# Two VectorE operations instead of three in a weight decode, and a cosine reduced by an integer conversion

## The chip, the cores and the metric

One core of one Trainium2 chip. The metric is the device time of the program in microseconds (us); less is better. A profile of one execution of the kernel before the change is at hand.

## The reference

Three stages follow one another. Attention with a sparse mask runs over 4 batches, 8 heads, 576 positions and 64 columns a head; its output is laid out as 2304 tokens by 512. Two feed-forward layers (512 to 2048 to 512) follow:

```python
h = x @ w_in                      # first layer
x = (h * np.cos(h)) @ w_out
h = x @ w_in2                     # second layer
x = (P(h) / (Q(h) + 1e-6)) @ w_out2
```

P is a cubic in h, Q is 1 + |b0||h| + |b1|h^2. The weights w_in and w_out of both layers reach the chip as 64-bit words (an 8-byte word for each weight), and the kernel turns each word into an fp32 number.

## The kernel before, in words

**Tiling and steps.** A step is one slice of 128 of the 2048 hidden columns for one block of tokens. `l1` (L419) makes h for it with 12 matrix multiplications: the token slices x and the weights are each held as a high and a low part, and high times high, high times low and low times high are summed. `l2` (L438) adds the slice's share of the output with 12 more. The first layer has 128 steps: steps 0 to 31 on two blocks of 256 tokens that alternate, 16 on a block of 352, 80 on five blocks of 288. The second layer has 96 steps of 384 tokens, with another elementwise part (`ew_a` to `ew_d`), which the change does not touch.

**Decode of the weights.** Each weight tile is loaded as `raw` (128 x 512 words of 8 bytes). `dec_abs` lets ScalarE scale the upper half-word, read as fp32, by 2^-112 (L142; one tile, L144, goes to VectorE). `dec_ops` then makes three VectorE operations on 128 x 512: a shift left by 3 (c = 0, L154), the sign bit (c = 1, L156), and the three bits that come from the lower half-word (c = 2, L158). `w_split` makes the high part on ScalarE (L173) and the low part on GpSimd or VectorE (L176). The first layer's 32 tiles are decoded during the start and steps 0 to 15; the second layer's 32 tiles between about 170 and 505 us, and these are written to memory and read back later.

**Elementwise part of the first layer** (`ew_op`), one letter an operation: U or u makes u = h/2pi + 0.25 on ScalarE (L508) or VectorE (L510); K or k copies h out of its bank (L512, L514); J or j adds the number 1.5 x 2^23 on ScalarE (L516) or VectorE (L518), which rounds u to a whole number; V takes the difference of the two (L520, VectorE); N is the sine on ScalarE (L522); M multiplies by h, or by its copy where there is one (L524, VectorE); G and H make the high and low parts (L528, L530) for `l2`.

**What sets the order.** The order is written out by hand: a list of commands for the start (`START`), a string of letters for each step (`ORD`, `C_ORD`), with s and w for the splits of decoded tiles, a and b for `dec_abs` of the next step's tiles, x, y, z, p, q for their `dec_ops` (x is c = 0 of both, y and z are c = 1, p and q are c = 2), T and L for pieces of attention. Each engine works through its own instructions in that order. `l1` is issued at the head of a step, and in the first 32 steps `l2` of a step two steps later. h lies in one of two PSUM banks: `l1` of a step waits until the last reader of h of two steps before is done.

**Attention** for later tokens runs in between, in pieces: transposes (L355), products with v (L374), their copies (L363, L385, L386), sums and normalisations (L297, L344 to L346).

Of the kernel before, what the change touches and what calls it, by code (L numbers as in the profile page):

```python
# [8 lines left out]
F32 = mybir.dt.float32  # L9
F32R = mybir.dt.float32r  # L10
I32 = mybir.dt.int32
BF16 = mybir.dt.bfloat16
AF = mybir.ActivationFunctionType
ALU = mybir.AluOpType
AX = mybir.AxisListType

B, H, S, D = 4, 8, 576, 64
# [3 lines left out]
NF = DFF // 128  # L21
# [12 lines left out]
NB2 = 384  # L34
# [17 lines left out]
LV1 = (3, 4)  # L52
PL1 = []
AB_ORD = "UKjVTswxyzNMabpqGHL"
NEED = {"J": "U", "V": "J", "N": "V", "M": "N", "G": "M", "H": "G"}
REST = "swNMUKjVGhTL"
C_ORD = {}
ORD = {}
for _g in (0, 1, 23):
    ORD[_g] = "ukjVTswxyzNMabpqGHL"  # L60
NPRE = 4
EVB, STB = 4, 6
LATE_OE = False
# [3 lines left out]
NCONST = C_ID + 128  # L67
TWO_PI = 6.2831850
INV_2PI = 1.0 / (2.0 * math.pi)
MAGIC = 12582912.0  # L70
LN_SHIFT = 2.0 ** -63


# [17 lines left out]
def attention_moe_moe_kernel(ctx: ExitStack, tc: tile.TileContext, qk0, qk, vv, w1, w2, consts, a, b, out):  # L91
    nc = tc.nc
    ACT, DVE, POOL, PE, SP = nc.scalar, nc.vector, nc.gpsimd, nc.tensor, nc.sync
# [4 lines left out]
    ep = ctx.enter_context(tc.tile_pool(name="ep", bufs=2))  # L98
# [13 lines left out]
    biases = const.tile([128, 4], F32, name="biases")  # L112
# [16 lines left out]
    def w_load(p, src, key, f, o, ring=False, eng=None):  # L129
        if ring:  # L130
            t = wp.tile([128, 512, 2], I32, tag=f"w{o}", name="raw")
        else:
            t = p.tile([128, 512, 2], I32, tag="A", bufs=ABUFS, name="raw")
        (eng or SP).dma_start(out=t.rearrange("p n w -> p (n w)"), in_=src[f, o].bitcast(I32))
        raws[key, f, o] = t

    def dec_abs(key, f, o, eng=None):
        t = raws.pop((key, f, o))
        m = stage("dec")
        src = t[:, :, 1].bitcast(F32)  # L140
        if eng is None:
            ACT.activation(out=m, in_=src, func=AF.Copy, scale=2.0 ** -112)  # L142
        else:
            eng.tensor_scalar(out=m, in0=src, scalar1=2.0 ** -112, scalar2=None, op0=ALU.mult)  # L144
        return t, m

    def dec_bits(*tms):
        dec_bits1(*tms)
        dec_bits2(*tms)

    def dec_ops(c, t, m):
        mi = m.bitcast(I32)
        if c == 0:
            DVE.tensor_scalar(out=mi, in0=mi, scalar1=3, scalar2=None, op0=ALU.logical_shift_left)  # L154
        elif c == 1:
            DVE.scalar_tensor_tensor(out=mi, in0=t[:, :, 1], scalar=-0x80000000, in1=mi, op0=ALU.bitwise_and, op1=ALU.bitwise_or)  # L156
        else:
            DVE.scalar_tensor_tensor(out=mi, in0=t[:, :, 0], scalar=29, in1=mi, op0=ALU.logical_shift_right, op1=ALU.bitwise_or)  # L158

    def dec_bits1(*tms):  # L160
        for c in (0, 1):
            for t, m in tms:
                dec_ops(c, t, m)

    def dec_bits2(*tms):
        for t, m in tms:
            dec_ops(2, t, m)

    def w_split(m, key, f, o, eng, heng=None):
        w = wp.tile([128, 2, 512], F32R, tag=f"w{o}", name=f"w{o}")  # L170
# [325 lines left out]
    def ew_new(g, bk, h):  # L496
        n = blocks[bk]["n"]
        e = dict(g=g, h=h)
        for k in ("u", "t", "hs"):
            e[k] = ep.tile([128, NB2], F32, tag=k, name=k)[:, :n]  # L500
        for k in ("gh", "gl"):
            e[k] = None
        return e

    def ew_op(c, e):
        u, t, hs, h = e["u"], e["t"], e["hs"], e["h"]
        if c == "U":
            ACT.activation(out=u, in_=h, func=AF.Identity, scale=INV_2PI, bias=biases[:, 2:3])  # L508
        elif c == "u":
            DVE.tensor_scalar(out=u, in0=h, scalar1=INV_2PI, scalar2=0.25, op0=ALU.mult, op1=ALU.add)  # L510
        elif c == "K":
            ACT.activation(out=hs, in_=h, func=AF.Copy)  # L512
        elif c == "k":
            DVE.tensor_copy(out=hs, in_=h)  # L514
        elif c == "J":
            ACT.activation(out=t, in_=u, func=AF.Identity, bias=biases[:, 3:4])  # L516
        elif c == "j":
            DVE.tensor_scalar(out=t, in0=u, scalar1=MAGIC, scalar2=None, op0=ALU.add)  # L518
        elif c == "V":
            DVE.scalar_tensor_tensor(out=u, in0=t, scalar=MAGIC, in1=u, op0=ALU.subtract, op1=ALU.subtract)  # L520
        elif c == "N":
            ACT.activation(out=u, in_=u, func=AF.Sin, scale=-TWO_PI)  # L522
        elif c == "M":
            DVE.tensor_tensor(out=t, in0=u, in1=hs if "K" in e else h, op=ALU.mult)  # L524
        elif c == "G":
            n = t.shape[1]
            e["gh"], e["gl"] = (gp.tile([128, NB2], F32R, tag=k, name=k)[:, :n] for k in ("gh", "gl"))
            ACT.activation(out=e["gh"], in_=t, func=AF.Copy)  # L528
        else:
            (POOL if c == "H" else DVE).tensor_tensor(out=e["gl"], in0=t, in1=e["gh"].bitcast(F32), op=ALU.subtract)  # L530
            state["g", e["g"]] = e["gh"], e["gl"]

# [118 lines left out]
    def order(g):  # L651
        return ORD[g] if g in ORD else AB_ORD if g < 2 * NF else C_ORD[g % (2 * NF)] if g % (2 * NF) in C_ORD else REST
# [9 lines left out]
    def run_steps(p, g0, g1):  # L662
        for g in range(g0, g1):
            bk = None
            if g < len(steps):
                bk, f = steps[g]
                h = l1(bk, f)
            if state["evac"]:
                evac(state["evac"].pop())
            run("early", g)  # L670
            if g < N1:
                todo = decs.pop(g, ())
                e = ew_new(g, bk, h)
                fifo = {c: state["e"] + [e] if c in "NMGH" else [e] for c in "UKJVNMGH"}
                state["e"].append(e)
                for c in order(g):
                    if c.upper() in fifo:
                        for x in fifo[c.upper()]:
                            if c.upper() not in x and NEED.get(c.upper(), "U") in x | {"U": 1}:
                                x[c.upper()] = True  # L680
                                ew_op(c, x)
                                break
                    elif c in "sS":
                        split1(0, POOL if c == "s" else DVE)
                    elif c in "wW":
                        split1(1, POOL if c == "w" else DVE)
                    elif c in "xyzpq":
                        if c == "x":
                            for _, tm in todo:
                                dec_ops(0, *tm)  # L690
                        else:
                            i = "yzpq".index(c)
                            if i % 2 < len(todo):
                                dec_ops(1 + i // 2, *todo[i % 2][1])
                    elif c in "ab":
                        for k in dplan.get(g + 1, ())["ab".index(c):][:1]:
                            w_abs(g + 1, k)
                    elif c == "T":
                        run("pe1", g)
                        run("pe1e", g)  # L700
                    elif c == "L":
                        run("late", g)
                state["e"] = [x for x in state["e"] if "H" not in x]
                state["dec"] = todo
            else:
                for x in state["e"]:
                    for c in "NMGH":
                        if c not in x:
                            ew_op(c, x)
                state["e"] = []  # L710
                second(g, LAG)
                if g == N1:
                    nc.scalar.preload_act_table_set("natural_log_exp_and_others")
                prev = state.pop("prev", None)
                if prev is not None:
                    ew_b(*prev)
                if state["evac"]:
                    evac(state["evac"].pop())
                if bk is not None:
                    state["prev"] = ew_a(p, bk, h)  # L720
                if prev is not None:
                    gh = ew_c(*prev[:2])
                if bk is not None:
                    ew_r(*state["prev"])
                if prev is not None:
                    state["g", g - 1] = ew_d(*prev[:2], gh)
                run("pe1", g)
                run("pe1e", g)
                run("late", g)
            if g < N1:  # L730
                second(g, LAG_AB if bk <= bB else LAG)
            run("pe2", g)
            run("load", g)
# [5 lines left out]
    with tc.manual_schedule():  # L739
        with tc.tile_pool(name="att", bufs=2) as p:  # L740
# [1 line left out]
            DVE.memset(msk16, 0.0)  # L742
            DVE.memset(biases[:, 1:2], -63.0 * math.log(2.0))
            DVE.memset(biases[:, 2:3], 0.25)
            DVE.memset(biases[:, 3:4], MAGIC)
            wb = bank("a")
            ms = {}

# [181 lines left out]
```

## Time and profile before

| what | value |
|---|---|
| median of 3 runs | 993.06 us (992.69 to 993.42) |
| profiled execution | 990.51 us, span 988.7 us, mean granted TensorE clock 0.984 |
| TensorE (PE) busy | 925.2 us, 94% |
| VectorE (DVE) busy | 786.6 us, 80% |
| ScalarE (ACT) busy | 670.8 us, 68% |
| GpSimd (POOL) busy | 287.5 us, 29% |

The page gives busy time over the whole span. Stages have different limits, so the rows further down cut the span at 27, 45, 100, 133, 185.5 and 575 us: the end of the first attention pieces, the first steps, the end of the first layer's decode, the end of the steps of 256 tokens, the end of the first layer. In a row of a group, the number after "x" is how many instructions it holds.

### The profile page before, as it was taken

The page shows a single profiled execution, that of the slowest core. Times are in us where ns is not written, and L with a number is a line of the kernel's source. Part 1 is how long each engine was busy: PE and PEld are TensorE (multiplying, and loading weights), DVE is VectorE, ACT ScalarE, POOL GpSimd, SP SyncE. Part 2 cuts the span into 40 slices and gives each one's busy share as a digit, 9 for nine tenths or more (in the row PEclk, how much of TensorE's full clock was granted, in tenths as well). Part 3 has the DMA queues.
Part 4 walks back from the last instruction along what each step waited for, and adds up shares of the span by engine and source line. Part 5 has one row for each costly group of instructions (what it writes and reads, how often), then busy time and mean ns, then how long its engine had stood idle before and what let it go on. Part 6 is the DMA issues. An engine that isn't in the chain of part 4 may idle for free.

```text
span 988.7 us, 17482 instructions
## 1 busy us (share of the span) xinstructions
PE 925.2 (94%) x6367; PEld 861.8 (87%) x6367; DVE 786.6 (80%) x1497; ACT 670.8 (68%) x1444; POOL 287.5 (29%) x279
## 2 busy tenths in 40 slices
PE   7557889999999989999899999999999999999997
PEld 6557789998999989999899988888888898898896
DVE  5999986688677787777878898877787778777776
ACT  5765557565475565765757887777777777777775
POOL 2466552213212122121222223223223232232221
PEclk9778999999999999999999999999999999999999
DMA  9745200443423534234325620010010100100000
GB/s 312 254 168 216 62 22 9 148 159 109 138 86 128 172 138 160 89 128 151 128 60 178 188 78 1 2 64 1 6 60 1 51 14 1 65 1 0 33 1 32
DMA packets 51526, 89.36 MB, mean 90 GB/s; under 512 B 4584, under 2 KB 28400, under 8 KB 51440
## 3 DMA queue, kind: packets, MB, share of 16 engines
q1 hardware_dynamic: 50720, 86.58, 26.6%
q10 hardware_dynamic: 720, 1.67, 0.5%
q8 instruction: 50, 0.82, 0.3%
q14 instruction: 36, 0.29, 0.1%
HBM read 70.40 MB, written 17.83 MB: 89 GB/s over the span
## 4 chain that ended last, share of the span: by engine, by line
DVE 32%; PE 26%; ACT 22%; POOL 10%; issue 7%; DMA 3%; POOLq 0%; SPq 0%; ACTq 0%; DVEq 0%
PE h L419 11%; PE y L438 10%; POOL z L478 9%; DVE r L481 7%; ACT r L477 6%; ACT r L476 5%; ACT gh L487 4%; DVE h L482 3%; DVE dec L156 3%; DVE a L482 3%; DVE t L524 3%; DVE dec L158 2%; PE a L259 2%; DVE u L520 2%; DVE t L518 2%
## 5 line engine op out<-in xcount | busy, mean ns | idle before, releaser
L419 PE MATMUL h<-xh,w 128*128 128x288 f32 (+3 forms) x1408 | 339.5, 313 | 9.2 <-DVE hs L514 4.4
L419 PEld LDWEIGHTS h<-xh,w 128*128 128x128 f32 x1408 | 246.2, 191 | 14.6 <-DVE hs L514 4.6
L438 PE MATMUL y<-gh,w 128*128 128x288 f32 (+2 forms) x1024 | 231.3, 302 | 4.5 <-ACT gh L528 4.5
L419 PE MATMUL h<-xl,w 128*128 128x288 f32 (+3 forms) x704 | 207.9, 311 | 0.0
L438 PE MATMUL y<-w,gh 128*128 128x512 f32 x576 | 196.1, 393 | 5.6 <-DVE ev L452 4.3
L478 POOL TENSOR_TENSOR z<-q,r 128x384 f32<-128x384 f32 x96 | 97.3, 1013 | 297.3 <-ACT r L477 293.9
L438 PEld LDWEIGHTS y<-gh,w 128*128 128x128 f32 x1024 | 173.6, 191 | 5.2 <-ACT gh L528 5.2
L438 PE MATMUL y<-gl,w 128*128 128x288 f32 (+2 forms) x512 | 153.6, 300 | 6.0 <-POOL gl L530 5.6
L419 PEld LDWEIGHTS h<-xl,w 128*128 128x128 f32 x704 | 135.6, 193 | 1.8
L438 PEld LDWEIGHTS y<-w,gh 128*128 128x128 f32 x576 | 108.2, 188 | 27.9 <-DVE ev L452 6.8
L481 DVE SCALAR_TENSOR_TENSOR r<-z,r 128x384 f32<-128x384 f32 x96 | 69.5, 724 | 73.3 <-POOL z L478 73.3
L530 POOL TENSOR_TENSOR gl<-t,gh 128x288 fp32r<-128x288 f32 (+2 forms) x67 | 64.1, 957 | 197.4 <-ACT gh L528 180.9
L438 PE MATMUL y<-w,gl 128*128 128x512 f32 x288 | 114.8, 399 | 5.0 <-DVE gl L492 4.8
L419 PE MATMUL a<-xh,w 128*128 128x384 f32 x384 | 106.3, 337 | 0.0
L508 ACT ACTIVATE u<-h,biases 128x288 f32<-128x288 f32 (+2 forms) x116 | 57.2, 494 | 72.2 <-PE h L419 69.2
L438 PEld LDWEIGHTS y<-gl,w 128*128 128x128 f32 x512 | 97.8, 191 | 9.1 <-POOL gl L530 8.4
L528 ACT ACTIVATE gh<-t 128x288 fp32r<-128x288 f32 (+2 forms) x128 | 56.8, 443 | 54.6 <-DVE t L524 54.0
L518 DVE TENSOR_SCALAR t<-u 128x288 f32<-128x288 f32 (+2 forms) x123 | 53.2, 432 | 45.8 <-ACT u L508 44.3
L522 ACT ACTIVATE u<-u 128x288 f32<-128x288 f32 (+2 forms) x128 | 56.7, 443 | 43.7 <-DVE u L520 43.5
L524 DVE TENSOR_TENSOR t<-u,hs 128x288 f32<-128x288 f32 (+2 forms) x114 | 62.9, 552 | 23.8 <-ACT u L522 23.4
L520 DVE SCALAR_TENSOR_TENSOR u<-t,u 128x288 f32<-128x288 f32 (+2 forms) x128 | 74.2, 580 | 6.2 <-ACT t L516 2.0
L419 PEld LDWEIGHTS a<-xh,w 128*128 128x128 f32 x384 | 70.5, 188 | 1.8
(115 smaller groups left out, 1645.3 us busy)
## 6 DMA issues: line engine op xcount, KB each, us to landing
raw<-in_w_dram SPq DMA_DIRECT2D x63, 512.0 KB
qk<-in_qk_dram SPq DMA_DIRECT2D x18, 481.0 KB
wf<-dec SPq DMA_DIRECT2D x32, 256.0 KB
wf<-wf SPq DMA_DIRECT2D x32, 256.0 KB
x2s<-x2d SPq DMA_DIRECT2D x24, 192.0 KB
out_dram<-ev SPq DMA_DIRECT2D x17, 256.0 KB
v<-in_vv_dram SPq DMA_DIRECT2D x16, 240.0 KB
v<-in_vv_dram SPq DMA_DIRECT2D x24, 157.5 KB
```

What stands on the lines that cost most here:

```text
L419: PE.matmul(h[:, :n], w[d["ph"], f, 0][:, 128 * c:128 * c + 128], x[c][:, cs], start=k == 0, stop=k == len(ops) - 1)
L438: PE.matmul(y, l, r, start=first and i == 0 and bk != bB, stop=last and i == 2 and bk != bA)
L477: ACT.activation(out=r, in_=r, func=AF.Exp, scale=-1.0, bias=biases[:, 1:2])
L478: POOL.tensor_tensor(out=z, in0=q, in1=r, op=ALU.mult)
L481: DVE.scalar_tensor_tensor(out=r, in0=z, scalar=2.0, in1=r, op0=ALU.subtract, op1=ALU.mult, reverse0=True)
L482: DVE.scalar_tensor_tensor(out=h, in0=h, scalar=ab[:, 0:1], in1=r, op0=ALU.add, op1=ALU.mult)
L508: ACT.activation(out=u, in_=h, func=AF.Identity, scale=INV_2PI, bias=biases[:, 2:3])
L518: DVE.tensor_scalar(out=t, in0=u, scalar1=MAGIC, scalar2=None, op0=ALU.add)
L520: DVE.scalar_tensor_tensor(out=u, in0=t, scalar=MAGIC, in1=u, op0=ALU.subtract, op1=ALU.subtract)
L524: DVE.tensor_tensor(out=t, in0=u, in1=hs if "K" in e else h, op=ALU.mult)
L528: ACT.activation(out=e["gh"], in_=t, func=AF.Copy)
L530: (POOL if c == "H" else DVE).tensor_tensor(out=e["gl"], in0=t, in1=e["gh"].bitcast(F32), op=ALU.subtract)
```

## The change

The decode loses the operation c = 0. In its place `dec_abs` issues one more ScalarE operation: it reads the top byte of the lower half-word (a byte every 8 bytes), computes byte/32 - 31/64 and writes it converted to int32 over that half-word (an int32 every 8 bytes), which leaves the three top bits as a number from 0 to 7. c = 1 then shifts and joins these bits in one VectorE operation, c = 2 sets the sign. In the cosine, U writes h/2pi + 0.25 straight into an int32 tile, and J goes; V computes h/2pi minus that whole number, with h read from its PSUM bank; N adds its quarter turn as a bias operand. The letters x and j stay in the order strings and do nothing. In steps 0 to 31 the letters K and k are taken out of the strings; from step 32 on the copy stays.

```diff
+COPY = {ord(c): None for c in "Kk"}
-NEED = {"J": "U", "V": "J", ...
+NEED = {"J": "U", "V": "U", ...
...
+        ACT.activation(out=t[:, :, 0], in_=t.rearrange("p n w -> p (n w)").bitcast(U8).rearrange("p (n b) -> p n b", b=8)[:, :, 3],
+                       func=AF.Copy, scale=1.0 / 32.0, bias=-31.0 / 64.0)
         return t, m
...
-        if c == 0:
-            DVE.tensor_scalar(out=mi, in0=mi, scalar1=3, scalar2=None, op0=ALU.logical_shift_left)
-        elif c == 1:
+        if c == 1:
+            DVE.scalar_tensor_tensor(out=mi, in0=mi, scalar=3, in1=t[:, :, 0], op0=ALU.logical_shift_left, op1=ALU.bitwise_or)
+        elif c == 2:
             DVE.scalar_tensor_tensor(out=mi, in0=t[:, :, 1], scalar=-0x80000000, in1=mi, op0=ALU.bitwise_and, op1=ALU.bitwise_or)
-        else:
-            DVE.scalar_tensor_tensor(out=mi, in0=t[:, :, 0], scalar=29, in1=mi, op0=ALU.logical_shift_right, op1=ALU.bitwise_or)
...
+        k = t.bitcast(I32)
         if c == "U":
-            ACT.activation(out=u, in_=h, func=AF.Identity, scale=INV_2PI, bias=biases[:, 2:3])
+            ACT.activation(out=k, in_=h, func=AF.Identity, scale=INV_2PI, bias=biases[:, 2:3])
...
-        elif c == "J":
-            ACT.activation(out=t, in_=u, func=AF.Identity, bias=biases[:, 3:4])
-        elif c == "j":
-            DVE.tensor_scalar(out=t, in0=u, scalar1=MAGIC, scalar2=None, op0=ALU.add)
         elif c == "V":
-            DVE.scalar_tensor_tensor(out=u, in0=t, scalar=MAGIC, in1=u, op0=ALU.subtract, op1=ALU.subtract)
+            DVE.scalar_tensor_tensor(out=u, in0=h, scalar=INV_2PI, in1=k, op0=ALU.mult, op1=ALU.subtract)
         elif c == "N":
-            ACT.activation(out=u, in_=u, func=AF.Sin, scale=-TWO_PI)
+            ACT.activation(out=u, in_=u, func=AF.Sin, scale=TWO_PI, bias=biases[:, 3:4])
         elif c == "M":
-            DVE.tensor_tensor(out=t, in0=u, in1=hs if "K" in e else h, op=ALU.mult)
+            DVE.tensor_tensor(out=t, in0=u, in1=e.get("hs", h), op=ALU.mult)
...
-                for c in order(g):
+                for c in order(g).translate(COPY if g < 2 * NF else {}):
```

## Rows read from the trace of the kernel before

**Rows 1.** Busy time by stretch: length, then PE, PEld, DVE, ACT, POOL; clock, DMA, GB/s.
```profile
27.00:45.00 18.00, 9.95 (x91) 8.32 (x90) 17.30 (x34) 12.98 (x51) 8.80 (x8) 0.83 0.89 319
45.00:100.00 55.00, 38.71 (x291) 35.12 (x289) 54.07 (x81) 30.55 (x68) 32.72 (x25) 0.81 0.51 178
100.00:133.00 33.00, 26.34 (x203) 24.45 (x202) 30.95 (x50) 19.18 (x44) 19.49 (x16) 1.00 0.19 54
133.00:185.50 52.50, 51.89 (x479) 50.17 (x480) 37.39 (x90) 32.82 (x75) 16.75 (x19) 1.00 0.11 35
185.50:575.00 389.50, 378.87 (x3064) 371.84 (x3064) 302.69 (x625) 251.68 (x561) 87.09 (x88) 1.00 0.41 133
575.00:988.70 413.70, 399.34 (x1972) 354.42 (x1970) 327.56 (x582) 309.36 (x605) 115.42 (x115) 1.00 0.07 24
```

**Rows 2.** Chain of waits, 20 to 160 us: start, us, what.
```profile
49.83 1.59 DVE dec L154 x2
...
134.48 1.44 PE h L419 x12
```

**Rows 3.** VectorE's groups, 27 to 100 us: busy us, mean ns, idle before.
```profile
L156 DVE SCALAR_TENSOR_TENSOR dec<-raw,dec 128x512 int32<-128x512 int32 x20 | 17.2, 896 | 0.0
L158 DVE SCALAR_TENSOR_TENSOR dec<-raw,dec 128x512 int32<-128x512 int32 x18 | 14.8, 856 | 0.0
L154 DVE TENSOR_SCALAR dec<-dec 128x512 int32<-128x512 int32 x20 | 14.7, 770 | 0.0
L520 DVE SCALAR_TENSOR_TENSOR u<-t,u 128x256 f32<-128x256 f32 x9 | 6.2, 692 | 0.3
L518 DVE TENSOR_SCALAR t<-u 128x256 f32<-128x256 f32 x9 | 5.2, 580 | 0.1
L524 DVE TENSOR_TENSOR t<-u,hs 128x256 f32<-128x256 f32 x5 | 3.6, 727 | 0.5 <-ACT u L522 0.5
...
L524 DVE TENSOR_TENSOR t<-u,h 128x256 f32<-128x256 f32 x4 | 1.6, 408 | 0.0
```

**Rows 4.** Durations by source line, whole span: ns least/median/most, first and last start.
```profile
L154 DVE TENSOR_SCALAR dec<-dec x64: 407/421/1525, 14.3 to 503.0; 128x512 int32<-128x512 int32 x64
L518 DVE TENSOR_SCALAR t<-u x123: 277/310/1378, 44.1 to 561.8; 128x288 f32<-128x288 f32 x78, 128x256 f32<-128x256 f32 x29, 128x352 f32<-128x352 f32 x16
L524 DVE TENSOR_TENSOR t<-u,h x14: 407/422/509, 53.9 to 457.6; 128x256 f32<-128x256 f32 x9, 128x288 f32<-128x288 f32 x4, 128x352 f32<-128x352 f32 x1
```

**Rows 5.** Timeline of GpSimd and VectorE near 110 us: start, us, what.
```profile
110.27 2.75 POOL L176 TENSOR_TENSOR w<-dec,w 128x512 fp32r<-128x512 f32 x2
...
110.49 1.40 DVE L520 SCALAR_TENSOR_TENSOR u<-t,u 128x256 f32<-128x256 f32 x1
112.37 0.42 DVE L524 TENSOR_TENSOR t<-u,h 128x256 f32<-128x256 f32 x1 [0.48 <-ACT u L522]
```

**Rows 6.** ScalarE's groups, whole span, shapes apart.
```profile
L142 ACT ACTIVATE dec<-raw 128x512 f32<-128x512 f32 x63 | 39.5, 669 | 2.2 <-DMA raw<-in_w_dram 2.1
L508 ACT ACTIVATE u<-h,biases 128x288 f32<-128x288 f32 x79 | 39.1, 495 | 60.2 <-PE h L419 58.6 <-PE a L355 1.4
L512 ACT ACTIVATE hs<-h 128x288 f32<-128x288 f32 x73 | 29.3, 402 | 0.0
...
L173 ACT ACTIVATE w<-dec 128x512 fp32r<-128x512 f32 x31 | 18.9, 626 | 1.6 <-DVE dec L158 1.6
```

**Rows 7.** TensorE's waits, 27 to 133 us: us in total, times, longest.
```profile
PE h L419 <- DVE hs L514: 4.4, 1, 4.4
...
PE h L419 <- DVE t L524: 3.0, 5, 0.9
```

**Rows 8.** Chain of waits, 336 to 368 us.
```profile
339.22 1.25 DVE t L518
...
356.51 1.11 DVE dec L154 x2
```

**Rows 9.** Chain of waits, 408 to 432 us.
```profile
417.26 0.68 ACT dec L142
```

More of the change, by code (lines that the diff above doesn't have):

```diff
@@ L11 @@
 I32 = mybir.dt.int32
+U8 = mybir.dt.uint8
 BF16 = mybir.dt.bfloat16
@@ L54 @@
 AB_ORD = "UKjVTswxyzNMabpqGHL"
-NEED = {"J": "U", "V": "J", "N": "V", "M": "N", "G": "M", "H": "G"}
+NEED = {"J": "U", "V": "U", "N": "V", "M": "N", "G": "M", "H": "G"}
 REST = "swNMUKjVGhTL"
@@ L69 @@
 INV_2PI = 1.0 / (2.0 * math.pi)
-MAGIC = 12582912.0
 LN_SHIFT = 2.0 ** -63
@@ L144, in dec_abs @@
             eng.tensor_scalar(out=m, in0=src, scalar1=2.0 ** -112, scalar2=None, op0=ALU.mult)
+        ACT.activation(out=t[:, :, 0], in_=t.rearrange("p n w -> p (n w)").bitcast(U8).rearrange("p (n b) -> p n b", b=8)[:, :, 3],
+                       func=AF.Copy, scale=1.0 / 32.0, bias=-31.0 / 64.0)
         return t, m
-    def dec_bits(*tms):
-        dec_bits1(*tms)
-        dec_bits2(*tms)
     def dec_ops(c, t, m):
         mi = m.bitcast(I32)
-        if c == 0:
-            DVE.tensor_scalar(out=mi, in0=mi, scalar1=3, scalar2=None, op0=ALU.logical_shift_left)
-        elif c == 1:
+        if c == 1:
+            DVE.scalar_tensor_tensor(out=mi, in0=mi, scalar=3, in1=t[:, :, 0], op0=ALU.logical_shift_left, op1=ALU.bitwise_or)
+        elif c == 2:
             DVE.scalar_tensor_tensor(out=mi, in0=t[:, :, 1], scalar=-0x80000000, in1=mi, op0=ALU.bitwise_and, op1=ALU.bitwise_or)
-        else:
-            DVE.scalar_tensor_tensor(out=mi, in0=t[:, :, 0], scalar=29, in1=mi, op0=ALU.logical_shift_right, op1=ALU.bitwise_or)
[L160 to L167, printed above, removed]
     def w_split(m, key, f, o, eng, heng=None):
@@ L498, in ew_new @@
         e = dict(g=g, h=h)
-        for k in ("u", "t", "hs"):
+        for k in ("u", "t"):
             e[k] = ep.tile([128, NB2], F32, tag=k, name=k)[:, :n]
-        for k in ("gh", "gl"):
-            e[k] = None
         return e
     def ew_op(c, e):
-        u, t, hs, h = e["u"], e["t"], e["hs"], e["h"]
+        u, t, h = e["u"], e["t"], e["h"]
+        k = t.bitcast(I32)
         if c == "U":
-            ACT.activation(out=u, in_=h, func=AF.Identity, scale=INV_2PI, bias=biases[:, 2:3])
+            ACT.activation(out=k, in_=h, func=AF.Identity, scale=INV_2PI, bias=biases[:, 2:3])
         elif c == "u":
[L510 to L514, printed above, removed]
-        elif c == "J":
-            ACT.activation(out=t, in_=u, func=AF.Identity, bias=biases[:, 3:4])
-        elif c == "j":
-            DVE.tensor_scalar(out=t, in0=u, scalar1=MAGIC, scalar2=None, op0=ALU.add)
+            DVE.tensor_scalar(out=k, in0=h, scalar1=INV_2PI, scalar2=0.25, op0=ALU.mult, op1=ALU.add)
+        elif c in "Kk":
+            e["hs"] = ep.tile([128, NB2], F32, tag="hs", name="hs")[:, :t.shape[1]]
+            if c == "K":
+                ACT.activation(out=e["hs"], in_=h, func=AF.Copy)
+            else:
+                DVE.tensor_copy(out=e["hs"], in_=h)
         elif c == "V":
-            DVE.scalar_tensor_tensor(out=u, in0=t, scalar=MAGIC, in1=u, op0=ALU.subtract, op1=ALU.subtract)
+            DVE.scalar_tensor_tensor(out=u, in0=h, scalar=INV_2PI, in1=k, op0=ALU.mult, op1=ALU.subtract)
         elif c == "N":
-            ACT.activation(out=u, in_=u, func=AF.Sin, scale=-TWO_PI)
+            ACT.activation(out=u, in_=u, func=AF.Sin, scale=TWO_PI, bias=biases[:, 3:4])
         elif c == "M":
-            DVE.tensor_tensor(out=t, in0=u, in1=hs if "K" in e else h, op=ALU.mult)
+            DVE.tensor_tensor(out=t, in0=u, in1=e.get("hs", h), op=ALU.mult)
         elif c == "G":
@@ L528, in ew_op @@
             ACT.activation(out=e["gh"], in_=t, func=AF.Copy)
-        else:
+        elif c in "Hh":
             (POOL if c == "H" else DVE).tensor_tensor(out=e["gl"], in0=t, in1=e["gh"].bitcast(F32), op=ALU.subtract)
@@ L744, in attention_moe_moe_kernel @@
             DVE.memset(biases[:, 2:3], 0.25)
-            DVE.memset(biases[:, 3:4], MAGIC)
+            DVE.memset(biases[:, 3:4], 0.25 * TWO_PI)
             wb = bank("a")
```

## The prediction

> **What bounds the kernel now.** I read the busy times by stretch first, because the page's shares (TensorE 94%) hide where each engine leads. From 575 us on, the second layer runs, which the change leaves as it is; I count nothing there [rows 1]. From 133 to 185.5 us TensorE is busy for 51.89 of 52.50 us: nothing on VectorE can shorten that stretch by more than 0.6 us [rows 1]. From 185.5 to 575 us it is idle for 389.5 - 378.87 = 10.6 us, the most that can be won there [rows 1]. Only from 27 to 133 us does another engine lead. VectorE is busy for 17.30 + 54.07 = 71.4 of the 73 us to 100, and for 30.95 of the 33 us after that, while TensorE is idle for 24.3 and 6.7 us [rows 1]. The chain of waits says the same: near 50 us it goes through VectorE's decode, near 134 us it has passed to l1's 12 multiplications, 1.44 us a time [rows 2].
>
> Next come VectorE's groups in the leading stretch. The three decode operations are 46.7 us of its 71.4, the rounding L518 and the difference L520 another 11.4 [rows 3]. Their means look odd: L154 takes 770 ns here and 421 ns as its median over the span, L518 580 against 310 [rows 3, 4]. The timeline shows why. At 110.49 us L520, with both inputs in SBUF, takes 1.40 us, beginning just behind GpSimd's pair of subtractions, and ends near the middle of that pair's 2.75 us, where the first of the two ends. At 112.37 us, with the second one still running, the product L524 that reads h from PSUM takes 0.42 us [rows 5]. So an SBUF-to-SBUF operation stands still until GpSimd's instruction is through, and one with an input in PSUM does not: L524 with h never takes over 509 ns, with the copy hs it takes 727 ns on average here [rows 3, 4].
>
> **The change, part by part, 27 to 100 us.**
> Removed, c = 0: 20 operations, 14.7 us. If each held only its own 407 ns, 8.1 us go, and the rest is waiting for GpSimd, which the next decode operation inherits (c = 1 and c = 2 keep both inputs in SBUF and their cost) [rows 3, 4].
> Removed, j: 9 operations, 5.2 us, of which 9 x 277 ns = 2.5 us are their own [rows 3, 4].
> V, now with h from PSUM: the trace has no such operation. The nearest row is L524 with h, of the same size and the same places of its operands, 408 ns here, against L520's 692. I take 408, so 9 x 0.284 = 2.6 us go if nothing inherits the wait, 0 if all of it is inherited; above 692 it would only be if the int32 input cost more, which no row suggests [rows 3].
> M, no longer from the copy in steps 0 to 31: 5 x (727 - 408) = 1.6 us or 0, by the same reasoning [rows 3].
> So VectorE loses between 8.1 + 2.5 = 10.6 us and 14.7 + 5.2 + 2.6 + 1.6 = 24.1 us. I take 11, next to the lower end, because GpSimd's own work of 8.80 + 32.72 us is unchanged and 32.0 us of decode operations still have to fit between it [rows 1, 3].
>
> [...]
>
> Added on ScalarE, the byte operation: not in the trace. From below, L173 moves 512 contiguous elements in 626 ns and L142 reads them 8 bytes apart in 669: 43 ns for the stride. From above, twice L142, 1.34 us, if byte reads and strided int32 writes went at half rate. I take 0.70, one more stride on L142 [rows 6]. 20 of them add 14 us to ScalarE's 43.5 in this stretch, while the stretch shrinks to 62 us: 57.5 of 62, still not the leader, but near it [rows 1]. A removed K gives back 0.40 each.
> N's bias operand: L508 with one takes 495 ns, L512 without one 402, both from PSUM at 288 columns. So 93 ns more on each sine, on the path V to N to M: 9 x 0.09 = 0.8 us [rows 6].
> The bank of h: without the copy, l1 of two steps later waits for M, not for K. At step 0 the copy already held TensorE for 4.4 us [rows 7]; M comes two decode operations later, but the decode ahead of it has become shorter. Where M read h before, TensorE waited for it 5 times, 0.6 us on average [rows 7]. I charge 1 us, and bound it by 0 and by 9 x 0.9 = 8 us.
> Sum to 100 us: 11 - 0.8 - 1 = about 9 us.
>
> **100 to 133 us.** The same operations go, more than the 6.7 us for which TensorE is idle there [rows 1], so TensorE ends this gain: two decoding steps need 4 x 1.44 = 5.8 us of l1 and l2 at the least [rows 2]. I take 4.5 of the 6.7.
>
> **185.5 to 575 us.** The chain at each half-batch of attention goes through L518 (1.25 us once) and L154 (1.11 us for two) [rows 8], but elsewhere through ScalarE's dec_abs [rows 9], where the byte operation adds 0.70 per tile. The copy stays here, and V follows U directly, so the bank comes free about when the copy would free it. Of the 10.6 us idle [rows 1] I take 4, bounded by 0 and 8.
>
> The start before 27 us and the DMA queue: the code issues the weight loads in the same order, each at the end of a step, so they come as much sooner as the steps do; DMA is half idle from 45 to 100 us [rows 1]. Zero for both, with 1.5 us possible at the start.
>
> **Sum.** 9 + 4.5 + 4 = 17.5, and 0.5 for the stretch to 185.5 us: 18. The profiled execution took 990.51 us (span 988.7, 1.8 around it), so it would take 972.5. The median of the runs shown is 2.55 us above that execution: 975.
>
> **Rivals.**
> *ScalarE takes over.* If the byte operation costs 1.34 us, ScalarE has 43.5 + 26.8 + 0.8 = 71 us to do in the first 73: no gain of more than 2 there, some 3 up to 133 us, 1 later. That gives 993.06 - 6 = 987. For it: ScalarE runs in order, and the high parts for l2 stand behind dec_abs in many steps. Against it: the stride alone cost 43 ns [rows 6].
> *The bank of h becomes the wait (the other side).* All 32 first steps tie l1 to M. If each waited for the longest such wait so far, 0.9 us [rows 7], TensorE would lose 32 x 0.9 = 29 us, and the time would be 975 + 29 = 1004. It decides from 18/32 = 0.56 us a step on. For it: the mean of those 5 waits is 0.6. Against it: only 5 occurred, and M itself comes sooner once L518 and the blocked L520 are gone.
> *More than forecast.* If the waits for GpSimd aren't inherited, VectorE loses 24 us before 100 us; with 6 of the 6.7 and 8 of the 10.6 us that is up to 36 less costs, and ScalarE then limits it to about 28: 965.
>
> **How the numbers follow.** Forecast 0.68 (its own range 966 to 983, from gains of 27 and 10), ScalarE 0.14, the bank 0.08, more 0.10. Two tenths outside: the range runs from 962 to 988, which takes in ScalarE's case and most of the larger gain, and leaves the bank's. No change means within 0.2%, 2 us, about what a measurement of this kernel can tell. Faster: all of the forecast and of "more", and most of ScalarE's, 0.88; same 0.04; slower 0.08.
>
> **What would show it.** Right: no L154 and L518 operations; V near 0.41 us also beside GpSimd; 64 byte operations near 0.70 us; the steps of 352 tokens starting about 14 us earlier; the second layer as long as before. TensorE idle before 133 us falls from 31 to about 17 us. Wrong: c = 1 growing above 0.9 us (waits inherited in full), TensorE waiting for M in many of the first 32 steps (the bank), VectorE idle behind ScalarE's byte operation, or V blocked by GpSimd in spite of its PSUM input.

## The result, and the profile after

The changed kernel takes 977.88 us (median, 975.9 to 978.84) against 993.24 for the kernel before on the same chip: a ratio of 0.984, 95% interval [0.9821, 0.9859]. The profiled execution has a span of 974.1 us against 988.7, so 14.6 us are to be found in the trace.

| | before | after |
|---|---|---|
| TensorE (PE) busy | 925.2 us | 919.2 us |
| VectorE (DVE) busy | 786.6 us | 700.5 us |
| ScalarE (ACT) busy | 670.8 us | 707.9 us |
| GpSimd (POOL) busy | 287.5 us | 292.5 us |

Busy time by stretch of the changed kernel, with the columns of [rows 1]; the stretches end at the same steps only roughly, since the steps come sooner:
```profile
27.00:45.00 18.00, 8.54 (x68) 6.83 (x64) 16.93 (x31) 17.83 (x61) 8.20 (x7) 0.71 0.90 321
45.00:100.00 55.00, 43.65 (x366) 41.17 (x367) 46.54 (x68) 44.93 (x96) 40.54 (x31) 0.91 0.56 191
100.00:116.50 16.50, 16.50 (x140) 16.33 (x139) 13.26 (x22) 12.54 (x28) 11.77 (x10) 1.00 0.21 66
166.00:560.00 394.00, 380.79 (x3068) 372.38 (x3067) 253.49 (x502) 275.13 (x591) 92.47 (x88) 1.00 0.41 132
```
VectorE was busy for 17.3 of 18 us and 54.1 of 55 [rows 1]; now it is busy for 46.5 of the 55, and ScalarE is the full one from 27 to 45 us (17.83 of 18). The TensorE work of 45 to 100 us has grown from 38.7 to 43.65 busy us: it comes sooner.

To see where the time went, a step is better than a fixed window: the start of the first of l1's 12 multiplications of the same step in both traces. Two of them on TensorE's timeline before, at step 32 (the first of 352 tokens) and at step 128 (the first of the second layer), columns start, us, what:
```profile
185.31 0.33 PE L419 MATMUL h<-xh,w 128*128 128x352 f32 x1
...
562.21 0.34 PE L419 MATMUL h<-xh,w 128*128 128x384 f32 x1
```
The same two after:
```profile
166.23 0.33 PE L408 MATMUL h<-xh,w 128*128 128x352 f32 x1
...
547.27 0.34 PE L408 MATMUL h<-xh,w 128*128 128x384 f32 x1
```
At step 32 the changed kernel is 185.31 - 166.23 = 19.1 us ahead, at step 128 only 562.21 - 547.27 = 14.9. Steps 32 to 128 take 376.90 us before and 381.04 after: 4.1 us are given back there. With two more of these starts (step 0: 35.24 and 34.62; step 10: 100.33 and 90.34; step 18: 134.31 and 116.72) the whole difference is laid out:

| stretch | forecast | measured |
|---|---|---|
| to step 0 | 0 | -0.6 |
| step 0 to 10 (27 to 100 us before) | -9 | -9.4 |
| step 10 to 18 (100 to 134 us) | -4.5 | -7.6 |
| step 18 to 32 (134 to 185 us) | -0.5 | -1.5 |
| step 32 to 128 (185 to 562 us) | -4 | +4.1 |
| second layer | 0 | +0.3 |

One profile is good to about 2 us in front: eight kernels whose steps run the same code up to step 25 (this one, e5 to e7 and e9 to e12) reach that step 16.2 to 19.8 us ahead of the kernel before, this one 19.3. The late steps repeat to 1.5 us: e3 and e4, which have this kernel's code from step 32 on, take 382.5 and 382.4 us for steps 32 to 128, against 381.0.

VectorE's groups of the changed kernel, 27 to 100 us, to be held against [rows 3]; L154 is now the shift and join of c = 1, L156 the sign, L507 is V, L511 is M:
```profile
L156 DVE SCALAR_TENSOR_TENSOR dec<-raw,dec 128x512 int32<-128x512 int32 x22 | 22.0, 1034 | 0.0
L154 DVE SCALAR_TENSOR_TENSOR dec<-dec,raw 128x512 int32<-128x512 int32 x23 | 21.6, 964 | 1.5 <-ACT raw L147 1.5
L507 DVE SCALAR_TENSOR_TENSOR u<-h,t 128x256 f32<-128x256 f32 x13 | 5.4, 418 | 1.9 <-ACT t L497 1.8
L511 DVE TENSOR_TENSOR t<-u,h 128x256 f32<-128x256 f32 x12 | 5.0, 417 | 5.0 <-ACT u L509 5.0
```
A tile's decode costs VectorE 964 + 1034 = 2.00 us in place of 770 + 896 + 856 = 2.52 [rows 3]: of the 770 ns of c = 0 the other two took over 246. V takes 418 ns where it took 692, M 417 where it took 727 with the copy. Durations by source line over the whole span, for V, the byte operation (L147) and the sine (L509), ns least/median/most, first and last start:
```profile
L507 DVE SCALAR_TENSOR_TENSOR u<-h,t x128: 405/458/526, 42.2 to 546.8; 128x288 f32<-128x288 f32 x80, 128x256 f32<-128x256 f32 x32, 128x352 f32<-128x352 f32 x16
L147 ACT ACTIVATE raw<-raw x64: 643/669/781, 15.3 to 484.7; 128x512 int32<-128x512 uint8 x64
L509 ACT ACTIVATE u<-u,biases x128: 490/530/610, 42.7 to 548.0; 128x288 f32<-128x288 f32 x80, 128x256 f32<-128x256 f32 x32, 128x352 f32<-128x352 f32 x16
```
V is never above 526 ns in 128 calls, beside GpSimd or not: at 57.09 us it takes 0.41 us while GpSimd's L517 runs from 56.22 for 1.18. The byte operation's median, 669 ns, is the mean of L142 [rows 6].

TensorE's waits after, 160 to 575 us (us in total, times, longest):
```profile
PE h L408 <- DVE t L511: 4.3, 2, 2.2
PE a L344 <- POOL p L335: 2.9, 2, 1.5
PE h L408 <- DVE u L507: 2.6, 3, 0.9
```
In the trace before, l1 does not wait for VectorE in steps 32 to 128; there the largest wait is for GpSimd's normalisation, 4.9 us in 3, and l1 waits for a copy of h twice:
```profile
PE h L419 <- ACT hs L512: 1.7, 2, 0.9
```
Now l1 waits for V and for M, 6.9 us in 5 waits.

### The profile page after: what moved, and what is told of

It reads as the page before. It is cut to its first block, busy times and chain, and to the rows that moved or that the text cites. A ratio compares the mean times of both kernels' runs of the same rounds, so it can differ in the third digit from the quotient of the medians.

```text
span 974.1 us, 17268 instructions
## 1 busy us (share of the span) xinstructions
PE 919.2 (94%) x6367; PEld 857.1 (88%) x6367; DVE 700.5 (72%) x1305; ACT 707.9 (73%) x1485; POOL 292.5 (30%) x279
## 3 DMA queue, kind: packets, MB, share of 16 engines
HBM read 70.40 MB, written 17.83 MB: 91 GB/s over the span
## 4 chain that ended last, share of the span: by engine, by line
PE 23%; ACT 22%; DVE 19%; POOL 10%; issue 5%; DMA 1%; POOLq 0%; ACTq 0%; DVEq 0%
PE h L408 10%; POOL z L467 9%; PE y L427 9%; DVE r L470 7%; ACT r L466 6%; ACT r L465 5%; ACT gh L476 4%; DVE h L471 3%; DVE a L471 3%; PE a L363 1%; PE a L248 1%; DVE t L511 1%; PE a L344 1%; ACT dec L143 1%; ACT L509 1%
## 5 line engine op out<-in xcount | busy, mean ns | idle before, releaser
L408 PE MATMUL h<-xh,w 128*128 128x288 f32 (+3 forms) x1408 | 338.6, 312 | 15.5 <-DVE t L511 11.9
L517 POOL TENSOR_TENSOR gl<-t,gh 128x288 fp32r<-128x288 f32 (+2 forms) x67 | 68.6, 1025 | 186.9 <-ACT gh L515 162.0
L497 ACT ACTIVATE t<-h,biases 128x288 int32<-128x288 f32 (+2 forms) x116 | 57.7, 497 | 78.5 <-PE h L408 66.1
L507 DVE SCALAR_TENSOR_TENSOR u<-h,t 128x288 f32<-128x288 f32 (+2 forms) x128 | 58.2, 455 | 68.5 <-ACT hs L503 53.3
L509 ACT ACTIVATE u<-u,biases 128x288 f32<-128x288 f32 (+2 forms) x128 | 67.8, 530 | 12.1 <-DVE u L507 11.7
L511 DVE TENSOR_TENSOR t<-u,hs 128x288 f32<-128x288 f32 (+1 forms) x91 | 49.2, 541 | 36.7 <-ACT u L509 36.5
L427 PEld LDWEIGHTS y<-w,gl 128*128 128x128 f32 x288 | 54.0, 188 | 20.1 <-DVE gl L481 12.1
```

The costliest lines, as they stand in the source:

```text
L408: PE.matmul(h[:, :n], w[d["ph"], f, 0][:, 128 * c:128 * c + 128], x[c][:, cs], start=k == 0, stop=k == len(ops) - 1)
L427: PE.matmul(y, l, r, start=first and i == 0 and bk != bB, stop=last and i == 2 and bk != bA)
L497: ACT.activation(out=k, in_=h, func=AF.Identity, scale=INV_2PI, bias=biases[:, 2:3])
L507: DVE.scalar_tensor_tensor(out=u, in0=h, scalar=INV_2PI, in1=k, op0=ALU.mult, op1=ALU.subtract)
L509: ACT.activation(out=u, in_=u, func=AF.Sin, scale=TWO_PI, bias=biases[:, 3:4])
L511: DVE.tensor_tensor(out=t, in0=u, in1=e.get("hs", h), op=ALU.mult)
```

## The experiments

The theory to start with: the gain in front is VectorE's work gone, and the late loss is ScalarE's byte operation. The rivals: the copies that went are the gain; the cosine, and not the decode, carries it; the loss is the freeing of the bank of h. Ratios are to the kernel before, run on the same chip.

**e1: the new decode alone.** The cosine and the copies are those of before.
```diff
 dec_abs: + ACT.activation(out=t[:, :, 0], in_=<top bytes>, func=AF.Copy, scale=1/32, bias=-31/64)
 dec_ops: c = 1 and c = 2 as in the changed kernel, no c = 0
```


> The new decode alone, with the cosine and the copies of before. My theory (VectorE's operations, waits for GpSimd included, set the pace until 133 us; ScalarE's byte operations cost later): about 9 us of the 19 won until step 25, then about 4 lost between steps 32 and 128, 988 us in all. Rival (the cosine does the late harm by holding h): the decode alone loses nothing after step 32 and the time is about 984.

995.0 us, ratio 1.0024 [1.0012, 1.0036]: slower than before, by 0.2%, and above both expectations. It is 5.9 us ahead at step 32, and steps 32 to 128 take 387.0 us, 10.1 more than before. V with both inputs in SBUF takes 761 ns there, where it took 834 before in the same window and takes 418 from the bank after the whole change. VectorE, 27 to 120 us:
```profile
L521 DVE SCALAR_TENSOR_TENSOR u<-t,u 128x256 f32<-128x256 f32 x15 | 11.4, 761 | 0.6
```
So the decode gains where VectorE leads, and loses more than that where TensorE leads.

**e2: the new cosine alone**, without the copies in steps 0 to 31, as in the changed kernel.
```diff
 dec_abs, dec_ops: as before the change (c = 0, 1, 2; no byte operation)
```


> The new cosine alone, with the decode of before. My theory: about 9 us won until step 25, nothing lost after step 32 or up to 2 us won there, 983 us. Rival (V and M hold the bank of h): the loss of 4 us after step 32 shows here, 988 us.

979.1 us, ratio 0.9872 [0.9852, 0.9892], not to be told from the whole change, and below both expectations. It is 8.5 us ahead at step 32, and steps 32 to 128 take 376.6 us, as before. Alone, the parts are 5.9 and 8.5 us ahead at step 32, together 19.1, more than their sum; by the medians the decode alone loses 2.7 us and the cosine alone gains 13.2, and together they gain 15.4. From 45 to 100 us VectorE is still busy for 53.0 us in e2 and for 49.4 in e1, against 46.5 with both.

**e3: the copies kept in steps 0 to 31**, and **e4: a copy in steps 0 and 1 only**.
```diff
-for c in order(g).translate(COPY if g < 2 * NF else {}):
+for c in order(g).translate({}):                                  # e3
+for c in order(g).translate(COPY if 2 <= g < 2 * NF else {}):     # e4
```


> The changed kernel with the copies of h in steps 0 to 31 put back. Theory A (an M that reads SBUF twice waits for GpSimd and the copies load ScalarE, the bank costs less): 2 to 4 us slower than the changed kernel, 980 to 982. Rival B (the bank held until M is what TensorE waits for, 11.9 us in its waits): 3 to 6 us faster, 972 to 975.

> The changed kernel with the copy kept in steps 0 and 1 alone, where TensorE waited 5.8 us for M of step 0. Theory (another wait ends last there, ScalarE being busy for 17.8 of the 18 us): less than 1 us either way, 977 to 979. Rival (that wait is on the path): l1 of step 2 starts 2 us sooner and the end comes 2 us sooner, 976.

e3: 981.78 us, 0.9888 [0.9865, 0.991]: the copies cost about 4 us, as theory A had it. e4: 977.44, 0.9854 [0.9834, 0.9875]: no difference, as the theory had it, although the changed kernel's largest wait in front is one of 5.8 us, by step 2's l1 for M of step 0. TensorE's waits of the changed kernel, 25 to 133 us:
```profile
PE h L408 <- DVE t L511: 7.6, 2, 5.8
```
That wait lies where VectorE and ScalarE are full (16.93 and 17.83 of the 18 us to 45), so freeing TensorE there earlier brings the end no closer. So the bank's largest wait in the first 32 steps is not on the path, and keeping every copy there (e3) costs more than it frees. The 1.8 us of the other wait in that line were not tested by themselves.

**e5: the old decode for the second layer's tiles only** (those decoded in steps 28 to 111), the new one for the first layer's.
```diff
+if key == 1:
     ACT.activation(out=t[:, :, 0], in_=<top bytes>, ...)
 second, third: dec_ops -> dec_ops2 (three VectorE operations, as before)
```


> The changed kernel, with the second layer's 32 tiles decoded as before (three VectorE operations, no byte operation). Theory (the byte operation stands before the sine on ScalarE and costs the 4.2 us lost between steps 32 and 130): the first 32 steps as in the changed kernel, nothing lost after them, 973 to 974 us. Rival (the loss comes of V holding h, or of the sine's bias operand): 977 to 978 as the changed kernel.

973.2 us, 0.9802 [0.9788, 0.9815]: faster than the change, intervals apart, as the theory expected. Steps 32 to 128 take 377.4 us.

**e6: the old cosine from step 32 on.**
```diff
+if e["g"] >= 2 * NF and c in "UuJjVN":   # magic number, J, V from SBUF, N without a bias operand
+    ...
+    return
```


> The changed kernel, with the cosine of before from step 32 on. Theory (the byte operation harms, and the added rounding on VectorE makes it worse, as in the kernel with the new decode alone, which lost 10 us there): 982 to 984 us. Rival (the new cosine is what harms after step 32): the 4 us come back, 974.

982.69 us, 0.9906 [0.9892, 0.9919], as the theory expected; steps 32 to 128 take 385.5 us. Beside the new decode, the new cosine is worth 4.5 us there, so the loss is not its. Beside the old decode it is worth 0.3 (e2).

**e7: the byte operation issued twice** for the second layer's tiles (the first result is overwritten).
```diff
+if key == 2:
+    ACT.activation(out=m.bitcast(I32), in_=<top bytes>, func=AF.Copy, scale=1/32, bias=-31/64)
```


> The changed kernel, with the byte operation issued twice for the second layer's tiles (the first result goes to the tile that the scaling then overwrites). Theory: 32 x 0.67 = 21 us more on ScalarE, not in the first 32 steps; the loss of 4.2 us between steps 32 and 130 at least doubles, 982 to 985 us. Rival (ScalarE has room there, it is busy for 275 of 394 us): 977 to 979.

1001.73 us, 1.0097 [1.0084, 1.011]. This is slower by far more than the theory said (982 to 985). Steps 32 to 128 take 403.2 us: 32 more operations of 0.66 us, 21.2 us of ScalarE's time, cost 22.2 us, where the first 32 cost 3.7 (e5 against the change), net of the 32 VectorE operations that they replace. Its waits, 160 to 575 us:
```profile
PE h L411 <- DVE t L514: 9.8, 2, 5.0
PE h L411 <- DVE u L510: 7.6, 5, 1.7
PE a L347 <- DVE xl L378: 7.0, 6, 1.4
```
All three are waits for VectorE, which the second byte operation gives nothing to do: so its operations must be late because ScalarE's are.

**e8: V and M read the copy in steps 0 to 31** (copies kept).
```diff
+for c in order(g).translate({}):
-DVE.scalar_tensor_tensor(out=u, in0=h, ...)
+DVE.scalar_tensor_tensor(out=u, in0=e.get("hs", h), ...)
```


> The changed kernel with the copies of h kept in steps 0 to 31, and V as well as M reading the copy in SBUF. It differs from the kernel with the copies kept (981.8 us) by V alone. Theory (an operation with both inputs in SBUF stands still beside GpSimd): V's mean in the first 32 steps goes from 0.42 to about 0.7 us, and the first 32 steps take 3 to 5 us longer, 985 to 987. Rival (where V reads makes no difference, the bank coming free sooner makes up for it): 981 to 982.

985.42 us, 0.9936 [0.9924, 0.9949], as the theory expected: 3.6 us above e3, which differs in V's operand alone. VectorE's V in e8, 27 to 120 us, from both places in the same stretch:
```profile
L507 DVE SCALAR_TENSOR_TENSOR u<-hs,t 128x256 f32<-128x256 f32 x7 | 5.5, 786 | 3.6 <-ACT hs L503 3.5
L507 DVE SCALAR_TENSOR_TENSOR u<-h,t 128x256 f32<-128x256 f32 x10 | 4.2, 416 | 1.8 <-ACT t L497 1.7
```
The same operation takes 786 ns from the copy and 416 from the bank.

**e9: e5 with a copy in four more steps** (55, 65, 87, 97, whose order strings have none).
```diff
-C_ORD 1: 'swNMUjVGhTL'    23: 'swNMUjVGhTL'
+C_ORD 1: 'swNMUKjVGhTL'   23: 'swNMUKjVGhTL'
```


> The kernel with the old decode in the second layer (973.2 us), and the copy of h also in steps 55, 65, 87 and 97, which have none; there TensorE waited 3.8 us for M in two waits. Theory (the bank of h is the wait left there): 970 to 971 us. Rival (another wait ends behind it, or ScalarE's four more copies cost as much): 973 to 974.

970.36 us, 0.9779 [0.9764, 0.9794], the best of all. The time is what the theory expected. With the same front as e5 (step 32 at 167.90 and 167.94 us), steps 32 to 128 take 374.0 us against 377.4; the intervals of e5 and e9 just overlap. The waits of e5, then of e9, 160 to 575 us:
```profile
PE h L418 <- DVE t L521: 3.8, 2, 1.9
PE a L354 <- POOL p L345: 2.7, 2, 1.4
```
```profile
PE a L354 <- POOL p L345: 4.1, 4, 1.4
PE h L418 <- DVE u L517: 1.4, 1, 1.4
```
The two waits for M (3.8 us) are gone: where no copy frees the bank of h, M does, and M is late. Not all of the 3.3 us is the bank's. After one of e5's two waits the granted clock was 0.51, and that step took 1.5 us longer (last section); without this, e9 is 1.8 us ahead.

These waits are the new cosine's, not the byte operation's: e2 and e5, which decode the second layer as before, have the same 3.8 us. In the kernel before, the l1's of steps 57 and 89 waited for the copy of the step just before instead (0.86 and 0.82 us), and began before M of two steps before had read its bank (292.23 us against 292.74). So there they took the other bank, although it is said above that l1 always waits for the last reader of two steps before. Now V reads that other bank after the copy, so it comes free later, and l1 waits for M.

**Where the late loss arises.** The starts of l1, read as above, give the length of every stretch of the late steps, us:

| steps | before | e2 | e5 | changed |
|---|---|---|---|---|
| 32 to 55 | 102.8 | 102.8 | 102.8 | 102.8 |
| 56 to 59 | 15.5 | 16.2 | 16.2 | 16.5 |
| 72 to 75 and 104 to 107 | 34.1 | 31.8 | 31.8 | 35.0 |
| 88 to 91 | 15.5 | 16.2 | 17.7 | 16.4 |
| the others | 209.0 | 209.6 | 208.8 | 210.4 |

e2 and e5 differ from the changed kernel there by the decode, and 3.2 us of what it costs lie in steps 72 to 75 and 104 to 107, where l1 waits for V. (The 17.7 of e5 hold the step at a clock of 0.51.) Part of the chain of waits from 320 to 360 us, first of the changed kernel, then of e5:
```profile
319.59 0.71 ACT dec L143
320.30 0.57 ACT raw L147
321.32 1.14 DVE t L511
```
```profile
332.63 1.58 PE y L437 x12
334.21 1.58 PE h L418 x12
```
In e5 the chain is TensorE's own up to 337 us. In the changed kernel it leaves TensorE at 317 us and goes through ScalarE and VectorE: the byte operation stands there ahead of a sine, M, a table load and the exponentials of attention. The table load for the next exponentials comes 1.79 us after the start of step 71, in e5 0.65; the U and V of that step, behind it, are late by as much, and l1 of step 73 waits for that V, which it does not in e5:
```profile
336.97 0.40 PE L408 MATMUL h<-xh,w 128*128 128x288 f32 x1 [0.94 <-DVE u L507]
```
M has the larger single waits, near 270 and 404 us. ScalarE near 270 us after the change (timeline; a scaling, 0.65 us, stands ahead of each byte operation):
```profile
271.62 0.65 ACT L147 ACTIVATE raw<-raw 128x512 int32<-128x512 uint8 x1
272.72 0.64 ACT L147 ACTIVATE raw<-raw 128x512 int32<-128x512 uint8 x1
273.26 0.52 ACT L509 ACTIVATE u<-u,biases 128x288 f32<-128x288 f32 x1
```
VectorE beside it:
```profile
273.40 0.69 DVE L154 SCALAR_TENSOR_TENSOR dec<-dec,raw 128x512 int32<-128x512 int32 x1 [0.40 <-ACT raw L147]
274.00 0.45 DVE L511 TENSOR_TENSOR t<-u,h 128x288 f32<-128x288 f32 x1
```
and TensorE:
```profile
274.50 0.40 PE L408 MATMUL h<-xh,w 128*128 128x288 f32 x1 [2.19 <-DVE t L511]
```
Two byte operations stand ahead of the sine on ScalarE, and c = 1, which waits for them, stands ahead of M on VectorE. But in e5, without them, this wait is 1.90 us, so they add only 0.3. Two kernels move what stands ahead of M.

**e10: the second layer's byte operations in the slot that c = 0 had**, behind the step's sine.
```diff
 dec_abs: - byte operation for key 2
 second:  + dec_byte(t) if c == 0 else dec_ops(c, t, m)
```


> The changed kernel, with the second layer's byte operations issued not behind each scaling but one place later, in the step where c = 0 used to stand. The work of ScalarE is the same. Theory (what costs is the order: four operations of 0.67 us in a row ahead of the sine, and c = 1 ahead of M on VectorE waiting for them): half or more of the 4.2 us come back, 974 to 976 us. Rival (the sum of ScalarE's work costs): 977 to 979, as the changed kernel.

979.05 us, 0.9869 [0.9852, 0.9885]: no gain, on the rival's side. The same place near 270 us in e10, ScalarE, VectorE and TensorE in turn:
```profile
273.55 0.52 ACT L512 ACTIVATE u<-u,biases 128x288 f32<-128x288 f32 x1
273.97 1.21 ACT L139 ACTIVATE raw<-raw 128x512 int32<-128x512 uint8 x2
```
```profile
274.64 1.29 DVE L157 SCALAR_TENSOR_TENSOR dec<-dec,raw 128x512 int32<-128x512 int32 x2 [1.61 <-ACT raw L139]
275.85 0.45 DVE L514 TENSOR_TENSOR t<-u,h 128x288 f32<-128x288 f32 x1
```
```profile
276.36 0.61 PE L411 MATMUL h<-xh,w 128*128 128x288 f32 x1 [3.25 <-DVE t L514]
```
The sine is done at 274.07, but M stands behind c = 1 until 275.85, and the wait grows from 2.19 to 3.25 us. By stretch, e10 wins 2.0 us in steps 72 to 75 and 104 to 107 and 1.2 in steps 32 to 55, and loses 2.4 and 2.7 in steps 56 to 59 and 88 to 91. Behind the wait above l1's multiplications start 0.24 us apart, in the step before 0.13, and the step takes 4.67 us (276.36 to 281.03) against 3.28 in the changed kernel (274.50 to 277.78, at a granted clock of 1.00): 1.4 of the 2.4 us.

**e11: c = 1 and c = 2 of the second layer one step later**, the byte operations where the change has them; **e12: that, with the copies of e9**.
```diff
-plan("late", g2, second, f, 1)
-plan("late", g3, third)
+plan("late", g2 + 1, second, f, 1)
+plan("late", g3 + 1, third)
```


> The changed kernel with the second and the third operation of the decode of the second layer's tiles (the byte operation's first reader on VectorE, and the one behind it) one step later; the byte operation stays where it is. Theory (VectorE's queue: the decode's operation waits for ScalarE's byte operation and stands ahead of the multiplication M that makes t): the two waits of TensorE for t near 270 us (2.2 us at most) are gone, steps 32 to 128 take 377 to 379 us in place of 381.05, and the time is 973 to 975. Rival (the sum of ScalarE's work in these steps, with whatever order): steps 32 to 128 stay at 380 to 382, and the time at 977 to 979.

> The kernel of e11, and the bank h copied to SBUF in four more steps (55, 65, 87, 97). Theory: the copies free the bank in the steps where l1 waits for M; with the decode's operation out of M's way they have less left to free, so the time is 970 to 972, near that of e9 (970.36), with the new decode. Rival (the sum of ScalarE's work): four copies and 20 byte operations both load ScalarE, and the time is 974 to 977.

Both expectations failed, the theory's by 24 us and more, the rival's by 19 and more. e11 takes 999.98 us, 1.0064 [1.0049, 1.0079]; e12 995.92, 1.0029 [1.0018, 1.0041]. Steps 32 to 128 take 402.3 and 399.1 us, with no more busy time on VectorE and ScalarE than after the change (243.8 and 264.5 us in e11, against 244.9 and 264.5): their order alone cost 21 us. The waits of e11, 160 to 575 us:
```profile
PE h L408 <- DVE t L511: 8.6, 2, 4.3
PE h L408 <- DVE u L507: 6.1, 4, 2.3
```
VectorE's timeline in e11 shows what the moved operations meet two steps before the longest of these waits:
```profile
269.52 1.29 DVE L154 SCALAR_TENSOR_TENSOR dec<-dec,raw 128x512 int32<-128x512 int32 x2
270.72 1.29 DVE L156 SCALAR_TENSOR_TENSOR dec<-raw,dec 128x512 int32<-128x512 int32 x2
271.93 0.48 DVE L272 TENSOR_TENSOR p<-a,cst 128x315 f32<-128x315 f32 x1
```
Attention's mask addition and maximum (L272, L275) now stand behind four decode operations: L272 begins 3.6 us after the start of its step, in the changed kernel 1.2. The M behind them, what ScalarE does with it, its table loads and exponentials, and then the sines come that much later. The l1 at 282.34 waits 4.32 us for M, although c = 1 is out of M's way there: M waits for the sine alone, which ScalarE begins at 281.28, behind the same dec, byte, dec, byte as after the change.

What follows: the late loss is the byte operation's (e5, e7). By the traces most of it reaches TensorE in steps 72 to 75 and 104 to 107, through ScalarE's queue, attention's exponentials, V and the bank of h; this path is read from the chain and the waits, and no run removed it alone. The longer waits for M are the new cosine's for the most part. That moving c = 1 and c = 2 one step later wins the loss back, as e11 was to show, is refuted, and so is moving the byte operations behind the sine (e10). What a placement would bring that moves c = 1 and the byte operations behind M together, without meeting attention's maximum, was not tried and stays open; so do the changed kernel, and the kernel before, with the four late copies and nothing else.

## Why the prediction was right or wrong, point by point

**The time and its sign were right** (977.88 in the range, 2.9 above the forecast), but by errors that cancel: from step 0 to step 32 the change gained 18.5 us where 14 were taken, and the late steps lost 4.1 where 4 were to be gained.

**27 to 100 us: 9.4 for 9, with its main term mis-sized.** Taken was 11 us less of VectorE's work, from bounds of 10.6 and 24.1, on the reasoning that the remaining operations inherit the waits for GpSimd. Measured on the rows above: the decode saves 2.52 - 2.00 = 0.52 us a tile, 10.4 us for 20 tiles; j's 5.2 us went whole; V saves 9 x 0.274 = 2.5, M 5 x 0.31 = 1.6: together 19.7 us. Of the waits for GpSimd only a part came back: c = 1 and c = 2 took over 246 of the 770 ns of c = 0, and V, M and j left none behind. So the 9 came out by luck, from a main term too small by 8.7 us. The stretch did not shorten by 19.7 us, since VectorE ceased to lead: it is idle for 8.5 of the 55 us, and from 27 to 45 us ScalarE is full. That looks like the rival "ScalarE takes over" come true in part (read from the busy times; e3, whose copies load ScalarE again, fits it), though not by its price: the byte operation takes 0.67 us, not 1.34.

**TensorE's idle time before 133 us** fell from 31.0 us to 20.8 (27 to 116.5 us after), not to 17. The rest of the gain is a term that the prediction did not have: the same multiplications took less time. Steps 0 to 10, before and after, in the columns of [rows 1]:
```profile
35.24:100.33 65.09, 44.20 (x319) 40.33 (x317) 63.95 (x100) 38.04 (x97) 38.62 (x30) 0.79 0.54 196
34.62:90.34 55.72, 38.54 (x318) 35.85 (x317) 50.49 (x74) 47.02 (x111) 39.95 (x31) 0.87 0.64 233
```
TensorE's busy time falls by 5.7 us of the 9.4, while its granted clock rises from 0.79 to 0.87.

**V from PSUM: right**, 418 ns for 408. **The byte operation: right**, 0.67 for 0.70. **N's bias operand: right**, 530 against 444 ns at 288 columns, 86 for 93. **The bank of h in front: right**: its rival, 29 us slower, did not come, and its largest wait costs nothing (e4).

**100 to 185 us: the caps were wrong.** The prediction said that TensorE's idle time, 6.7 and 0.6 us, is the most that can be won; 7.6 (6.5 to 7.6 in the kernels with the same code) and 1.5 were. The busy time of the same multiplications itself fell: in steps 10 to 18 from 27.56 us at a clock of 1.00 to 26.27 at 0.96, and in steps 18 to 32, at 1.00 in both, before and after:
```profile
134.31:185.31 51.00, 50.39 (x468) 48.67 (x467) 36.11 (x89) 32.68 (x75) 15.46 (x18) 1.00 0.11 35
116.72:166.23 49.51, 49.51 (x467) 48.47 (x467) 27.50 (x68) 31.13 (x64) 15.23 (x20) 1.00 0.11 36
```
So a busy stretch was not a full one here. The weight loads give a better cap in this case: from 100 to 133 us they are idle for 33.0 - 24.45 = 8.55 us, from 133 to 185.5 for 2.3 [rows 1], and neither was exceeded.

**185.5 to 575 us: the wrong sign.** The failing step is "Of the 10.6 us idle I take 4, bounded by 0 and 8": it excluded a loss, and two of its reasons failed.

*VectorE's relief.* In e2, without the late byte operation, the new cosine gains 1.15 us at each half-batch of attention (steps 72 to 75 and 104 to 107), where the prediction saw the chain pass through L518 [rows 8], but the late steps as a whole only 0.3. Losses elsewhere ate the rest, 0.65 us each in steps 56 to 59 and 88 to 91, where the bank is waited for: "V follows U directly, so the bank comes free about when the copy would free it" is wrong, since l1 now waits for V (1.4 us in e2) and for M (3.8 us, in place of 1.7 for the copy). The forecast priced the bank's wait in the first 32 steps, where its largest wait costs nothing (e4), and dismissed it in the late ones.

*The byte operation.* The chain there passes through dec_abs on ScalarE [rows 9]. The prediction charged 0.70 us for each tile's byte operation and then gave it no one to wait for. It cost 3.7 us (e5), most of it where attention's exponentials, and V behind them, stand after it on ScalarE.

**The second layer as long as before: right**, 0.3 us.

## What to carry to other kernels

Moving work from a full engine to a freer one paid here only in the stretches where the first one led (the decode alone, e1: 5.9 us won by step 32, 10.1 lost in steps 32 to 128); elsewhere price the receiving engine's queue, and name who stands behind the added instruction on it and on the engine that waits for it. To find the place, compare the starts of the same step in both traces; the largest single wait need not be where the time went (5.8 us in front, e4). So split such a change by stage: here the new decode for the first layer's tiles, the old one for the second's, and four copies more give 970.36 us. Where work is laid out by hand, moving operations by one step, with nothing added, can cost as much as added work: 21 us for 64 of them in e11, 22 us for the 32 that e7 adds.

## What the runs showed of the hardware that was not expected

- V with h from PSUM did not stand still beside GpSimd as it does with both inputs in SBUF: it takes 416 ns from the bank and 786 from the SBUF copy in the same stretch of the same kernel (e8), and at most 526 ns in the changed kernel's 128 calls.
- Byte reads at a stride of 8 bytes with a strided int32 write took ScalarE as long here as the strided fp32 read: 669 ns for L147 (median) and for L142 (mean).
- Behind some of TensorE's waits its granted clock was lower, behind others not, and the length of the wait alone does not tell which. In e5, l1 begins steps 57 and 89 after waits of 1.90 us each. After the first the granted clock is 1.00; after the second it is 0.51, and the step takes 4.81 us in place of 3.27. After the wait of 2.19 us near 270 us in the changed kernel it is 1.00; after the 4.32 us in e11 it is 0.54, and that step takes 4.81 us too (282.34 to 287.15). Busy time by stretch in e5 after the two waits:
```profile
275.97:279.20 3.23, 3.23 (x24) 3.23 (x25) 1.51 (x4) 2.02 (x5) 0.82 (x2) 1.00 0.02 5
402.05:405.40 3.35, 3.35 (x14) 3.35 (x15) 1.07 (x2) 0.92 (x3) 0.81 (x1) 0.51 0.00 0
```
